# Attention with a pooled branch, then a two-layer network: early output by transposes into one bf16 bank, the band mask added in PSUM, a new set of planner costs

## The chip, the cores and the metric

The kernel runs on one core of one Trainium2 chip. Times are device microseconds of one execution; lower is better. Engines are called by their profile names: PE (TensorE matmul), PEld (its weight loads), DVE (VectorE), ACT (ScalarE), POOL (GpSimd), SP (SyncE, which issues DMAs).

## The reference

Eight batches of eight heads, 576 positions, 64 channels. Each head has a local attention (each position sees the positions less than 4 away) and an attention over q, k and v averaged in groups of four, whose output is repeated four times. The two are added, the heads joined, and a two-layer network follows on all 4608 tokens.

```python
q_d = q.reshape(B, H, Sd, 4, D).mean(axis=3)          # k_d, v_d alike; Sd = 144
out_up = np.repeat(sm_attn(q_d, k_d, v_d), 4, axis=2)
mask = np.abs(pos[:, None] - pos[None, :]) < 4
scores = np.where(mask, scale * q @ k.T, -1e9)
out_local = softmax(scores) @ v
x = (out_up + out_local).transpose(0, 2, 1, 3).reshape(4608, 512)
h = x @ w_in                                          # 512 -> 2048
out = (h - np.tanh(h)) @ w_out                        # 2048 -> 512
```

## The kernel before, in words

Work is split into 32 pairs of heads, p = 0 to 31, four to a batch (NP = 4), and nine dense blocks of 512 tokens.

For a pair, q and k are loaded in float32 (`qkn`), cast and reordered to bf16 (`qr`, lines 515 and 523), and transposed so that channels lie on partitions: for p < 12 on PE (line 547) with a copy to `qk` (551), from p = 12 on by a transposing DMA into `qT` and an ACT copy (534). Two additions, on DVE or POOL (564, 569), sum groups of four into `qkd`. Windows of v are cast to bf16 (`vw`, 451); v is pooled by a matmul with `pick` for p < 12 and by POOL (472, 476) from then on.

The scores stand in PSUM. The local ones are made in five tiles of 120 or 96 queries by 128 keys (584): four tiles in the first two-bank buffer, t1, by `s1`; the fifth, with the pooled scores (606), in a second one, t2, by `s2`. From p = 12 on `s1` and `s2` are one operation. ACT takes exponentials into `E` (622 for t1; 634 and 637 for t2). For p < 4 the mask enters as a bias that PE adds (589). For the other 28 pairs DVE multiplies the exponentials, in SBUF, by a mask of ones and zeros (626 and 641). PE then multiplies `E` by v with a column of ones (650, 657), which gives the outputs and their sums in a third two-bank buffer; DVE takes the reciprocal (670) and scales (672) into `ln`, seven blocks: five local, two pooled.

What follows is the output step. For p < 12 (below `X_DMA`), `back` brings the channels to partitions and joins the parts on PE: three matmuls with the constant `up` spread each pooled column over four (683, 685), and six with the identity add the local part (692), all in a float32 buffer of two banks; a copy on DVE or ACT (720, 721) writes `xT`. From p = 12 on a transposing DMA on SP writes `lT`, and the `join`, two additions on DVE or POOL (703, 709), writes `xT`.

A dense block is 16 steps of `mm1` (734: four matmuls of 512 columns, then tanh on ACT, 742, and a subtraction on DVE into `gT`, 745) and 16 quarter steps of `mm2` (760: four matmuls each, sixteen for 128 rows of the result; then an ACT copy into `y`, 771, and a DMA out, 774). Steps of one block's `mm2` alternate with the next block's `mm1`.

The order is written by a planner. Each operation has an engine, a cost in ns, the things it reads and writes, and a priority; some have a choice of engine. `order` runs a list schedule with these costs, with latencies `LAT` after which another engine sees a result, and with eight PSUM banks of which a kind of work may hold so many (`cap`: attention "b" 6, dense "d" 4). On each engine the operation with the least priority number among the ready ones goes first; dense matmuls have 5000, attention 10p, so attention goes ahead of dense work on PE. The instructions of each engine then stand in a fixed order and wait by semaphores. Planned times aren't used on the chip. `filler` puts idle matmuls (911) in planned gaps of the start phase.

The exponential and the mask that follows it are these lines:

```python
op("ACT", 960, lambda: A.activation(
    out=e1, in_=two(t1)[:, :, 0:480], func=AF.Exp, scale=SCALE), drain=[t1], ...)
if p >= NP:
    op("DVE", 950, lambda: V.tensor_tensor(
        out=e1, in0=e1, in1=mask[:, 0:480].unsqueeze(1).to_broadcast([128, 2, 480]),
        op=ALU.mult), reads=["mask"], writes=[("E", e, 0)], pri=pri)
```

Of the kernel before, what the change touches and what calls it, by code (L numbers as in the profile page):

```python
# [23 lines left out]
class Program:  # L24

    LAT = {"PE": 270, "ACT": 150, "DVE": 110, "POOL": 150, "SP": 50, "DMA": 2200}
    RING = 230

    def __init__(self):
        self.ops = []  # L30
        self.alternatives = {}
        self.slack = []
        self.soon = set()
        self.goal = set()
        self.ring = {}
        self.rings = {}
        self.touch = []
        self.use = []
        self.toks = []
        self.cap = {}  # L40
        self.last_write = {}
        self.readers = {}
# [66 lines left out]
    def order(self):  # L109
# [56 lines left out]
        for i in range(n):  # L166
            if left[i] == 0:
                make_ready(i)
        for step in range(n):
            best = None  # L170
            for eng, cand in ready.items():
                if not cand:
                    continue
                now = max(free.get(eng, 0.0), min(at[i] for i in cand))
                if eng == "PE":
# [8 lines left out]
                else:  # L184
                    pick = min((self.ops[i][4], i) for i in cand if at[i] <= now)[1]
# [12 lines left out]
            end = now + self.ops[i][1]  # L198
            want = [t for t in self.use[i] if t.first == i]
# [57 lines left out]
def kernel(  # L257
# [9 lines left out]
    nc = tc.nc  # L267
# [31 lines left out]
    mask = fixed("mask", [128, 576], BF16)  # L299
# [19 lines left out]
    up = lT[1].rearrange("p n c -> p (n c)")[:, 0:S]  # L319
    r = fixed("r", [128, 2, 7], FP32, 2)  # L320
    ln = fixed("ln", [128, 7, 128], BF16, 2)
# [31 lines left out]
    def c_up():  # L353

        GP.memset(up, 1.0)
        GP.affine_select(out=up, in_=up, compare_op=ALU.is_ge, fill=0.0,
                         base=0, pattern=[[1, S]], channel_multiplier=-4)
        GP.affine_select(out=up, in_=up, compare_op=ALU.is_ge, fill=0.0,
                         base=3, pattern=[[-1, S]], channel_multiplier=4)

# [8 lines left out]
    def c_mask():  # L369

        GP.memset(mask, 1.0)
        m4 = mask[:, 0:480].rearrange("p (t c) -> p t c", c=QW)
        for part, pat in ((m4, [[0, 4], [1, QW]]),
                          (mask[:, 480:576], [[1, 96]])):
            neg = [[-s, n] for s, n in pat]
            GP.affine_select(
                out=part, in_=part, compare_op=ALU.is_ge, fill=0.0,
                base=-1, pattern=neg, channel_multiplier=1)
            GP.affine_select(
                out=part, in_=part, compare_op=ALU.is_ge, fill=0.0,  # L380
                base=7, pattern=pat, channel_multiplier=-1)
        GP.affine_select(
            out=mask[:, 0:QW], in_=mask[:, 0:QW], compare_op=ALU.is_ge,
            fill=0.0, base=-4, pattern=[[0, QW]], channel_multiplier=1)
        GP.affine_select(
            out=mask[:, 480:576], in_=mask[:, 480:576], compare_op=ALU.is_ge,
            fill=0.0, base=99, pattern=[[0, 96]], channel_multiplier=-1)
# [80 lines left out]
    def pool_v4(p):  # L468
# [9 lines left out]
        op("POOL", 1150, a1, reads=[("v4", s)], writes=["v2"], pri=10 * p - 12)  # L478
        op("POOL", 750, a2, reads=["v2"], writes=[("vp", s)], pri=10 * p - 12)

    def pool_v(hb):
# [15 lines left out]
        op("ACT", 590, lambda: A.copy(  # L497
# [5 lines left out]
    def attention(p):  # L503
# [10 lines left out]
        if p >= NEARLY:  # L514
            op("POOL", 1300, lambda: GP.tensor_copy(  # L515
# [14 lines left out]
        if p >= T_DMA:  # L530
            P.dma("SP", 1740, lambda: nc.sync.dma_start_transpose(
                out=qT[s], in_=qr[s].rearrange("p a c -> p (a c)")), 1300, 72,
                  src=[("qr", s, 0), ("qr", s, 1)], dst=[("qT", s)], pri=-50, lead=500)
            op("ACT", 1250, lambda: A.copy(  # L534
# [3 lines left out]
        else:  # L538
            for a0, a1, tn, cn in ((0, 5, 290, 740), (5, 9, 230, 620)):
# [10 lines left out]
                def copy(fn, a0=a0, a1=a1, b16=b16):  # L550
# [5 lines left out]
                          ("DVE", cn, lambda copy=copy: copy(V.tensor_copy))][:1 + (p < NP)],  # L556
# [10 lines left out]
        def add2(eng):  # L567
            with nc.allow_low_precision("pooled q and k"):
                eng.tensor_tensor(out=qkd[s][:, 0:G],  # L569
                                  in0=half[:, :, 0, :],  # L570
                                  in1=half[:, :, 1, :], op=ALU.add)
        P.choice([(name, n1, lambda eng=eng: add1(eng)) for name, n1, _, eng in adders],
# [41 lines left out]
        if new:  # L614
            op("PE", 620, s12, slack=late, reads=qks + [("qkd", s)], fill=[t1, t2], pri=pri)
        else:
            op("PE", 420 * cold + 250 * (p < NP), s1, slack=late,
# [4 lines left out]
        op("ACT", 960, lambda: A.activation(  # L622
            out=e1, in_=two(t1)[:, :, 0:480], func=AF.Exp, scale=SCALE),
           drain=[t1], writes=[("E", e, 0)], pri=pri)
        if p >= NP:
            op("DVE", 950, lambda: V.tensor_tensor(  # L626
                out=e1, in0=e1,
                in1=mask[:, 0:480].unsqueeze(1).to_broadcast([128, 2, 480]),
                op=ALU.mult), reads=["mask"], writes=[("E", e, 0)], pri=pri)
        yield  # L630
        if not new:
            op("PE", 380 * cold + 100 * (p < NP), s2, slack=late, reads=qks + [("qkd", s)],
               fill=[t2], pri=pri)
        op("ACT", 310, lambda: A.activation(  # L634
            out=e2v, in_=two(t2)[:, :, 0:96], func=AF.Exp, scale=SCALE),
           drain=[t2], writes=[("E", e, 1)], pri=pri)
        op("ACT", 650, lambda: A.activation(  # L637
            out=e3, in_=two(t2)[:, :, 96:384], func=AF.Exp, scale=SCALE / 16.0),
           drain=[t2], writes=[("E", e, 2)], pri=pri)
        if p >= NP:  # L640
            op("DVE", 450, lambda: V.tensor_tensor(  # L641
                out=e2v, in0=e2v,
                in1=mask[:, 480:576].unsqueeze(1).to_broadcast([128, 2, 96]),
                op=ALU.mult), reads=["mask"], writes=[("E", e, 1)], pri=pri)
# [25 lines left out]
        op("DVE", 200, lambda: V.reciprocal(out=r[s], in_=blocks()[:, :, :, 64]),  # L670
           drain=[to], writes=[("r", s)], pri=pri)
        op("DVE", 1060, lambda: V.tensor_tensor(  # L672
# [6 lines left out]
        tb = P.psum(2, kind)  # L679

        def back():
            for half in range(2):
                T.matmul(two(tb)[:, half, 0:288], ln[s][:, 5, :], up[:, 288 * half:288 * half + 288],
                         start=True, stop=False)
            T.matmul(two(tb)[:, 1, 224:288], ln[s][0:16, 6, :], up[0:16, 0:64],
                     start=False, stop=False)
            for t in range(NT):
                q0, q1 = QW * t, QW * t + NQ[t]
                for half in range(2):
                    c0, c1 = max(q0, 288 * half), min(q1, 288 * half + 288)  # L690
                    if c0 < c1:
                        T.matmul(two(tb)[:, half, c0 - 288 * half:c1 - 288 * half],  # L692
                                 ln[s][0:NQ[t], t, :], ident[0:NQ[t], c0 - q0:c1 - q0],
                                 start=False, stop=(t == (2, NT - 1)[half]))
        if p >= X_DMA:
            P.dma("SP", 1350, lambda: nc.sync.dma_start_transpose(
# [4 lines left out]
            def join(eng):  # L701
# [12 lines left out]
            P.choice([("DVE", 1900, lambda: join(V)), ("POOL", 1400, lambda: join(GP))],  # L714
                     reads=[("lT", s)], writes=[("x", b, j)], pri=pri)
            return
        op("PE", 450 * cold, back, slack=late, reads=[("ln", s), ("lT", 1), "ident"],
           fill=[tb], pri=pri)
        xs = xT[j][:, b * S:(b + 1) * S].rearrange("p (n c) -> p n c", n=2)
        P.choice([("DVE", 720, lambda: V.tensor_copy(out=xs, in_=two(tb)[:, :, 0:288])),  # L720
                  ("ACT", 680, lambda: A.copy(out=xs, in_=two(tb)[:, :, 0:288]))],
                 drain=[tb], writes=[("x", b, j)], pri=pri)
# [4 lines left out]
    def mm1(kb, fc):  # L727
# [14 lines left out]
        op("ACT", 590, lambda: A.activation(  # L742
            out=u[us], in_=one(tok), func=AF.Tanh),
           drain=[tok], writes=[("u", us)], pri=DPRI)
        op("DVE", 670, lambda: V.tensor_tensor(  # L745
# [6 lines left out]
    def mm2(kb, i):  # L752
        ts, part, g = i // 4, i % 4, kb % 2
        if part == 0:
# [190 lines left out]
```

The softmax here doesn't subtract the row's maximum and nothing guards it: scores larger than these inputs give would overflow.

## Time and profile before

| | us |
|---|---|
| median of 6 runs | 334.29 (331.36 to 335.60) |
| the profiled execution | 334.08, span 332.0 |
| PE busy | 317.8 (96%) |
| DVE busy | 211.6 (64%) |
| ACT busy | 202.6 (61%) |
| POOL busy | 176.6 (53%) |

The span goes from the first to the last instruction of the profiled execution; about 2 us of its own time lie around it. Busy times are of that execution. A matmul's busy time includes its way through the array, and the next one starts before it has ended, so a busy PE isn't PE at its best; idle PE time is certain. Until about 25 us the first batch's attention runs alone; dense matmuls go from 25.4 to 327.7 us, attention beside them until 249 us.

### The profile page before, as it was taken

Reading aid. Unit: us, or ns where it says so; the run is one execution under the profiler, and the core shown is the slowest. Engines: PE = TensorE matmul, PEld = TensorE weight load, DVE = VectorE, ACT = ScalarE, POOL = GpSimd, SP = SyncE. Lnnn points to the kernel's source line nnn. Section 1 sums busy time; section 2 is a strip of 40 time slices with the busy share of each in tenths; the row PEclk is TensorE's granted clock in tenths of the full one; section 3 lists DMA queues with packets and bytes.
Section 4 is the critical chain, followed back from the end, with each engine's and each line's share of the span. In section 5 each row is a group of like instructions: output and inputs, shape, how many; then the busy total and the mean of one; then the engine's idle time right before and its main releaser. Section 6 shows DMA issues by size and latency. Waiting matters only on the chain.

```text
span 332.0 us, 6546 instructions
## 1 busy us (share of the span) xinstructions
PE 317.8 (96%) x2461; PEld 158.6 (48%) x2461; DVE 211.6 (64%) x330; ACT 202.6 (61%) x334; POOL 176.6 (53%) x211
## 2 busy tenths in 40 slices
PE   7989999999999999999796999999999999999994
PEld 2554555564444544444443445444444444444441
DVE  4766764579967969777979868778754334443300
ACT  4878864588777866687764476868534443344411
POOL 8564448859667698879788848887310000000000
PEclk9999999999999999999999999999999999999999
DMA  7999999999999989999999999982320001000121
GB/s 235 252 244 206 250 253 229 315 307 220 251 261 259 248 189 241 259 215 239 237 244 230 270 224 255 199 214 61 91 59 34 32 33 64 32 32 32 37 92 64
DMA packets 108862, 59.80 MB, mean 180 GB/s; under 512 B 86174, under 2 KB 96030, under 8 KB 108830
## 3 DMA queue, kind: packets, MB, share of 16 engines
q1 hardware_dynamic: 104318, 54.60, 70.0%
q0 software_dynamic: 4224, 4.19, 7.7%
q10 hardware_dynamic: 288, 0.59, 0.6%
q8 instruction: 19, 0.31, 0.4%
q14 instruction: 13, 0.11, 0.1%
HBM read 43.64 MB, written 9.44 MB: 160 GB/s over the span
## 4 chain that ended last, share of the span: by engine, by line
PE 70%; DVE 13%; DMA 8%; ACT 3%; POOL 3%; issue 1%; SPq 1%; POOLq 0%; ACTq 0%
PE bank L760 32%; PE bank L734 28%; DMA vst<-in_v_dram 5%; DMA lT<-ln 3%; DVE E L626 3%; DVE E L641 3%; DVE ln L672 3%; PE bank L650 2%; PE bank L584 2%; DVE gT L745 2%; PE bank L657 2%; DVE xT L703 1%; ACT E L622 1%; PE bank L692 1%; PE bank L547 1%
## 5 line engine op out<-in xcount | busy, mean ns | idle before, releaser
L734 PE MATMUL bank<-xT,w_in_sb 128*128 128x512 bf16 x576 | 146.0, 379 | 0.3 <-DVE gT L745 0.3
L760 PE MATMUL bank<-w_out_sb,gT 128*128 128x512 bf16 x576 | 145.2, 379 | 0.0
L745 DVE TENSOR_TENSOR gT<-bank,u 128x512 bf16<-128x512 f32 x144 | 97.4, 685 | 63.3 <-ACT u L742 62.7
L742 ACT ACTIVATE u<-bank 128x512 f32<-128x512 f32 x144 | 86.0, 598 | 77.9 <-PE bank L734 75.3
L760 PEld LDWEIGHTS <-gT 128*128 128x128 bf16 x576 | 53.9, 98 | 62.0
L734 PEld LDWEIGHTS <-w_in_sb 128*128 128x128 bf16 x576 | 53.8, 98 | 62.0 <-issue 0.5
L564 POOL TENSOR_TENSOR half<-qk 128x576 f32<-128x576 bf16 x28 | 32.1, 1146 | 19.5 <-ACT qk L551 10.1
L515 POOL CAST qr<-qkn 128x1152 bf16<-128x1152 f32 x28 | 32.3, 1152 | 11.6 <-DMA qT<-qr 5.7
L622 ACT ACTIVATE E<-bank 128x960 bf16<-128x960 f32 x32 | 31.1, 972 | 11.9 <-PE bank L584 11.8
L626 DVE TENSOR_TENSOR E<-E,mask 128x960 bf16<-128x960 bf16 x28 | 30.3, 1082 | 11.3 <-ACT E L622 11.2
L672 DVE TENSOR_TENSOR ln<-bank,r 128x896 bf16<-128x896 f32 x32 | 34.7, 1087 | 0.9
L771 ACT COPY y<-bank 128x512 f32<-128x512 f32 x36 | 21.1, 587 | 19.6 <-PE bank L760 18.2
L451 POOL CAST vw<-vst 128x640 bf16<-128x640 f32 x31 | 25.3, 821 | 6.6 <-DMA vst<-in_v_dram 6.6
L472 POOL TENSOR_TENSOR v<-v 72x512 f32<-72x512 f32 x20 | 25.5, 1273 | 2.6 <-DMA v<-in_v_dram 1.9
L534 ACT COPY qk<-qT 128x1152 bf16<-128x1152 bf16 x20 | 24.1, 1204 | 1.7 <-DMA qT<-qr 1.7
L650 PE MATMUL bank<-vw,E 128*128 128x65 bf16 x320 | 20.1, 194 | 4.0 <-DVE E L641 2.2
L569 POOL TENSOR_TENSOR qkd<-half 128x288 bf16<-128x288 f32 x29 | 21.3, 735 | 1.3 <-DVE r L670 0.4
L650 PEld LDWEIGHTS <-E 128*128 128x128 bf16 x320 | 16.5, 98 | 11.1 <-DVE E L641 2.9
L476 POOL TENSOR_TENSOR vp<-v 72x256 bf16<-72x256 f32 x20 | 14.6, 732 | 12.8 <-PE bank L657 12.6
L637 ACT ACTIVATE E<-bank 128x576 bf16<-128x576 f32 x32 | 21.1, 660 | 0.0
L703 POOL TENSOR_TENSOR xT<-lT 128x480 bf16<-128x480 bf16 x11 | 11.1, 1010 | 15.3 <-DMA lT<-ln 15.2
L641 DVE TENSOR_TENSOR E<-E,mask 128x192 bf16<-128x192 bf16 x28 | 17.3, 618 | 0.7 <-ACT E L634 0.7
(75 smaller groups left out, 223.5 us busy)
## 6 DMA issues: line engine op xcount, KB each, us to landing
vst<-in_v_dram SPq DMA_DIRECT2D x62, 160.0 KB, 5.2
qkn<-in_q_dram SPq DMA_DIRECT2D x32, 288.0 KB, 5.7
out_dram<-y SPq DMA_DIRECT2D x36, 256.0 KB, 4.7
qkn<-in_k_dram SPq DMA_DIRECT2D x30, 288.0 KB, 5.8
v<-in_v_dram SPq DMA_DIRECT2D x20, 288.0 KB
w_in_sb<-in_moe_w_in_dram POOLq DMA_DIRECT2D x4, 512.0 KB, 13.1
w_out_sb<-in_moe_w_out_dram POOLq DMA_DIRECT2D x4, 512.0 KB, 9.1
qkn<-in_k_dram ACTq DMA_DIRECT2D x2, 288.0 KB, 3.3
```

Source lines behind the costliest of these rows:

```text
L472: GP.tensor_tensor(out=v2, in0=v4[s][:, :, :, 0:128], in1=v4[s][:, :, :, 128:256], op=ALU.add)
L515: op("POOL", 1300, lambda: GP.tensor_copy(out=qr[s].rearrange("p a (h d) -> p h a d", h=2), in_=qkn[sn].rearrange("p h (a d) -> p h a d", ...
L564: eng.tensor_tensor(out=half, in0=four[:, :, 0:2, :], in1=four[:, :, 2:4, :], op=ALU.add)
L622: op("ACT", 960, lambda: A.activation(out=e1, in_=two(t1)[:, :, 0:480], func=AF.Exp, scale=SCALE), drain=[t1], writes=[("E", e, 0)], pri=pri)
L626: op("DVE", 950, lambda: V.tensor_tensor(out=e1, in0=e1, in1=mask[:, 0:480].unsqueeze(1).to_broadcast([128, 2, 480]), op=ALU.mult), reads= ...
L641: op("DVE", 450, lambda: V.tensor_tensor(out=e2v, in0=e2v, in1=mask[:, 480:576].unsqueeze(1).to_broadcast([128, 2, 96]), op=ALU.mult), rea ...
L650: T.matmul(two(to)[:, hh, 65 * t:65 * t + 65], E[e][:, c:c + 128], vw[w][:, 2 * jj + hh, t, :], start=True, stop=True)
L672: op("DVE", 1060, lambda: V.tensor_tensor(out=ln[s].rearrange("p n (h d) -> p h n d", d=D), in0=blocks()[:, :, :, 0:64], in1=r[s].unsqueez ...
L734: T.matmul(one(tok), w_in_sb[:, dc, fc * 128:(fc + 1) * 128], xT[dc][:, kb * 512:kb * 512 + 512], start=(dc == 0), stop=(dc == N_DC - 1))
L742: op("ACT", 590, lambda: A.activation(out=u[us], in_=one(tok), func=AF.Tanh), drain=[tok], writes=[("u", us)], pri=DPRI)
L745: op("DVE", 670, lambda: V.tensor_tensor(out=gT[g][:, fc, :], in0=one(tok), in1=u[us], op=ALU.subtract), drain=[tok], reads=[("u", us)], w ...
L760: T.matmul(one(tok), gT[g][:, fc, ts * 128:ts * 128 + 128], w_out_sb[:, fc, :], start=(fc == 0), stop=(fc == N_FF - 1))
```

## The change

Six things change.

- For the 28 pairs p >= 4 the band is no longer multiplied into `E`. `bias` (0 in the band, -32768 outside) is added by DVE to the scores in PSUM, in place, before the exponential: one addition of 2 x 480 on t1, one of 2 x 96 on t2. `mask` is gone; POOL makes `bias` itself (`c_bias`).
- For p < 12 `back` is seven transposes on PE into one bank, read as bf16: five local blocks (576 columns) and two pooled ones (144). The pooled columns are copied into a new tile `od` by DVE or ACT, and DVE adds them, each spread over four, to the local ones from PSUM into `xT`. The constant `up` and `c_up` (three POOL operations) are gone.
- From p = 12 on the join may run on POOL only. Casts of v for p >= 4 may also run on ACT.
- Costs and latencies of the planner are new, and it keeps POOL apart from the DVE operations named in `port` (the additions 564 and 569).
- `s1` and `s2` are one operation from p = 8 on (`MERGE`). Results of `mm2` have a PSUM kind of their own, "y", with up to 3 banks.
- The last 128 rows of the last block are made in two halves of 256 columns, each with its own copy and DMA.

```diff
-    LAT = {"PE": 270, "ACT": 150, "DVE": 110, "POOL": 150, "SP": 50, "DMA": 2200}
+    LAT = {"PE": 235, "ACT": 145, "DVE": 110, "POOL": 140, "SP": 50, "DMA": 2000}
...
+                if eng == "DVE":
+                    now = max(free.get(eng, 0.0), min(
+                        max(at[i], port) if i in self.port else at[i] for i in cand))
+                elif eng == "POOL":
+                    now = max(now, port)
...
+            if eng == "POOL" or eng == "DVE" and i in self.port:
+                port = end
...
-    def c_mask():
+    def c_bias():
 
-        GP.memset(mask, 1.0)
+        GP.memset(bias, 0.0)
...
-        if new:
-            op("PE", 620, s12, slack=late, reads=qks + [("qkd", s)], fill=[t1, t2], pri=pri)
+        if p >= MERGE:
+            op("PE", 590, s12, slack=late, reads=qks + [("qkd", s)], fill=[t1, t2], pri=pri)
...
-        op("ACT", 960, lambda: A.activation(
+        def band(tok, lo, hi):
+            part = two(tok)[:, :, 0:hi - lo]
+            V.tensor_tensor(out=part, in0=part, in1=bias[:, lo:hi].unsqueeze(1)
+                            .to_broadcast([128, 2, hi - lo]), op=ALU.add)
+        if p >= NP:
+            op("DVE", 1080, lambda: band(t1, 0, 480), reads=["bias"], fill=[t1], pri=pri)
+        op("ACT", 860, lambda: A.activation(
...
         if p >= NP:
-            op("DVE", 950, lambda: V.tensor_tensor(
-                out=e1, in0=e1,
-                in1=mask[:, 0:480].unsqueeze(1).to_broadcast([128, 2, 480]),
-                op=ALU.mult), reads=["mask"], writes=[("E", e, 0)], pri=pri)
...
+            op("DVE", 280, lambda: band(t2, 480, 576), reads=["bias"], fill=[t2], pri=pri)
...
-        tb = P.psum(2, kind)
+        tb = P.psum(1, kind)
...
         def back():
-            for half in range(2):
-                T.matmul(two(tb)[:, half, 0:288], ln[s][:, 5, :], up[:, 288 * half:288 * half + 288],
-                         start=True, stop=False)
-            T.matmul(two(tb)[:, 1, 224:288], ln[s][0:16, 6, :], up[0:16, 0:64],
-                     start=False, stop=False)
...
+            for t in range(7):
+                q0, n = (QW * t, NQ[t]) if t < NT else (S + 128 * (t - NT), (128, 16)[t - NT])
+                T.transpose(flat()[:, q0:q0 + n], ln[s][0:n, t, :], ident[0:n, 0:n])
...
-            P.choice([("DVE", 1900, lambda: join(V)), ("POOL", 1400, lambda: join(GP))],
+            P.choice([("POOL", 1310, lambda: join(GP))],
...
-        P.choice([("DVE", 720, lambda: V.tensor_copy(out=xs, in_=two(tb)[:, :, 0:288])),
-                  ("ACT", 680, lambda: A.copy(out=xs, in_=two(tb)[:, :, 0:288]))],
-                 drain=[tb], writes=[("x", b, j)], pri=pri)
+        P.choice([("DVE", 130, lambda: V.tensor_copy(out=od[s], in_=flat()[:, S:S + G])),
+                  ("ACT", 170, lambda: A.copy(out=od[s], in_=flat()[:, S:S + G]))],
+                 drain=[tb], writes=[("od", s)], pri=pri)
+        op("DVE", 610, lambda: V.tensor_tensor(
+            out=xT[j][:, b * S:(b + 1) * S].rearrange("p (g a) -> p g a", a=4),
+            in0=flat()[:, 0:S].rearrange("p (g a) -> p g a", a=4),
+            in1=od[s].unsqueeze(2).to_broadcast([128, G, 4]), op=ALU.add),
+           drain=[tb], reads=[("od", s)], writes=[("x", b, j)], pri=pri)
...
-        op("DVE", 670, lambda: V.tensor_tensor(
+        op("DVE", 610, lambda: V.tensor_tensor(
             out=gT[g][:, fc, :], in0=one(tok), in1=u[us], op=ALU.subtract),
...
-        if part == 0:
-            ycur[0] = P.psum(1, "d")
+        split = kb == NBLK - 1 and ts == 3
+        if split:
+            cols, first, fcs = 256 * (part // 2), part % 2 == 0, 8
+        else:
+            cols, first, fcs = 0, part == 0, 4
+        if first:
+            ycur[0] = P.psum(1, "y")
...
+    MERGE = 8
...
-    T_QK, T_V, T_W, W_PRI, NEARLY = 800, 1000, 2850, 32, NP
-    CAST_V = [[("POOL", 820, GP.tensor_copy), ("ACT", 640, A.copy)],
-              [("POOL", 820, GP.tensor_copy)]]
+    T_QK, T_V, T_W, W_PRI, NEARLY = 760, 850, 3000, 32, NP
+    CAST_V = [[("POOL", 770, GP.tensor_copy), ("ACT", 620, A.copy)],
+              [("POOL", 770, GP.tensor_copy), ("ACT", 620, A.copy)]]
...
-    P.cap = {"b": 6, "d": 4}
+    P.cap = {"b": 6, "d": 4, "y": 3}
```

## The prediction, made before the changed kernel was run

> **What bounds the kernel now.** I read the page first (busy shares), then the table of windows, then what TensorE (PE) waits for, then the rows and spreads of the operations that the diff touches, and last the timeline of the worst stall. In the table of windows the columns are the window, its length, then busy time (instructions) of each engine, the clock and the DMA share.
>
> ```profile
> PE 317.8 (96%) x2461; PEld 158.6 (48%) x2461; DVE 211.6 (64%) x330; ACT 202.6 (61%) x334; POOL 176.6 (53%) x211
> ```
>
> ```profile
> 100.00:150.00 50.00, 49.45 (x388) 24.14 (x387) 40.04 (x56) 36.24 (x58) 40.12 (x45) 1.00 1.08 235
> 150.00:200.00 50.00, 45.47 (x371) 22.48 (x370) 40.93 (x55) 32.09 (x51) 39.53 (x43) 1.00 1.14 241
> 200.00:328.00 128.00, 127.68 (x767) 59.93 (x763) 63.18 (x94) 62.96 (x106) 30.36 (x36) 1.00 0.32 82
> sum 303.00, PE 296.95 PEld 146.28 DVE 195.96 ACT 185.67 POOL 159.46; mean PE 74.24 PEld 36.57 DVE 48.99 ACT 46.42 POOL 39.87
> ```
>
> The sum takes in 25 to 100 us as well. From 25 us, when the dense layers start, to 328 us PE is busy for 296.95 of 303 us, so the time after 25 us is PE's work plus about 6 us of holes, 4.5 of them between 150 and 200 us. In the timeline dense matmuls start 0.216 us apart; 1152 of them are 249 us, which no part of this change shortens. What can move is PE's attention work, the holes, the 25 us before and the 4 us after. Attention is not the bound: it ends before 249 us, and 80 us of dense work stand behind it.
>
> Who makes the holes (waits of PE from 25 to 328 us: total us, times, longest):
>
> ```profile
> PE bank L650 <- DVE E L641: 2.2, 2, 1.5
> PE bank L650 <- DVE gT L745: 1.1, 1, 1.1
> PE bank L606 <- POOL qkd L569: 1.1, 1, 1.1
> PE bank L650 <- DVE E L626: 0.5, 1, 0.5
> PE bank L683 <- DVE ln L672: 0.3, 1, 0.3
> PE bank L734 <- DVE gT L745: 0.3, 1, 0.3
> ```
>
> Five of the six are waits for VectorE (DVE), which is only 64% busy. The spreads (min/median/max ns, first and last start) say why:
>
> ```profile
> L626 DVE TENSOR_TENSOR E<-E,mask x28: 642/672/3476, 26.4 to 239.5; 128x960 bf16<-128x960 bf16 x28
> L641 DVE TENSOR_TENSOR E<-E,mask x28: 241/248/3804, 27.7 to 241.2; 128x192 bf16<-128x192 bf16 x28
> ```
>
> ```profile
> L703 DVE TENSOR_TENSOR xT<-lT x9: 646/1026/2992, 107.1 to 236.1; 128x480 bf16<-128x480 bf16 x9
> ```
>
> ```profile
> L745 DVE TENSOR_TENSOR gT<-bank,u x144: 627/691/693, 27.1 to 313.7; 128x512 bf16<-128x512 f32 x144
> ```
>
> Operations with both inputs in SBUF (the mask products L626 and L641, the join L703) stretch up to fifteen times; those with one input in PSUM (L745; L672 by its spread too, 1027 to 1093) never do. In the timeline (start us, us, engine, idle before) the longest stretch lies exactly beside a row of GpSimd (POOL) work:
>
> ```profile
> 177.16 1.01 POOL L703 TENSOR_TENSOR xT<-lT 128x480 bf16<-128x480 bf16 x1
> 177.20 3.80 DVE L641 TENSOR_TENSOR E<-E,mask 128x192 bf16<-128x192 bf16 x1
> ...
> 181.06 0.20 PE L650 MATMUL bank<-vw,E 128*128 128x65 bf16 x1 [1.54 <-DVE E L641]
> ```
>
> A 0.25 us product, begun 0.04 us behind a join on POOL, ends at 181.0, when POOL's unbroken row ends (join, two casts of v, a cast of qr until 180.9); PE, in order, stands behind it.
>
> **What the Trainium skill says.** "SBUF — State Buffer", section Who interferes with whom: DVE and GpSimd share one pair of SBUF ports as an exclusive lock; a DVE instruction with two SBUF inputs contends with a GpSimd instruction that reads SBUF, one with at most one SBUF input doesn't. The rows above agree: 3804 ns against 248 for the first kind, 693 against 691 for the second. "VectorE: DVE Perf Modes", The perf-mode tier table: tensor_tensor runs at 2x for bf16 in SBUF and at 1x with a PSUM operand. Agreed: 672 ns for 960 elements in SBUF, 1091 for 896 from PSUM. "TensorE: Matmul & The Clock Gate", Part 4: PE-mode transpose: about 275 ns in a kernel for a transpose; here L547 shows 219 ns for one and 56 ns from start to start, so the trace's spacing is used.
>
> **The change part by part.** All against the profiled execution: 334.08 us, of which the span is 332.0. The median of the runs is 334.29, so the difference carries over as it stands.
>
> 1. *Band added in PSUM (p >= 4).* L626 and L641 go: 30.3 + 17.3 = 47.6 us of DVE for 28 pairs, of which only 28 x (0.672 + 0.248) = 25.8 is their own work; 21.8 us is being locked out. In their place come two adds in PSUM before the exponentials. No row has DVE writing PSUM; the nearest are L672 (896 elements, 1087 ns) and L745 (512, 685), 1.05 ns an element: 960 elements 1.15 us, 192 elements 0.35, 42 us in all. Below: 1.0 us if a PSUM target is quicker; above: 1.3 if it is slower. So DVE gains only some 5 us of busy time, but the new operations have one SBUF input and can't be locked out. The chain per pair is now scores, add, exp, where it was scores, exp, mask: 1.15 + 0.35 against 0.67 + 0.25, 0.6 us longer undisturbed. That is covered by dense matmuls placed between; without this cover it would be 28 x 0.6 = 17 us.
>
> 2. *Joins on POOL alone (p >= 12).* The nine on DVE (9 x (1415 + 705) = 19 us) leave; POOL gets 9 x (1.01 + 0.35) = 12 us, and may give v casts (0.73 us each) to ScalarE (ACT). DVE has then no operation with two SBUF inputs after the start phase. Holes that hang on it: 2.2 + 1.1 (gT queued behind the 2.99 us join at 156.7) + 0.5 + 0.3 (gT behind a 2.25 us L626 at 81.8) = 4.1. Of the 1.1 for qkd, 0.4 is the same lock from the other side: that L569 took 1.08 us where 0.67 is usual. Together 4.5 us go.
>
> 3. *Early output (p < 12).* The old form is nine matmuls:
>
> ```profile
> 44.15 0.41 PE L683 MATMUL bank<-lT,ln 128*128 128x288 bf16 x2
> 44.49 0.20 PE L685 MATMUL bank<-lT,ln 16*128 16x64 bf16 x1
> 44.62 0.43 PE L692 MATMUL bank<-ident,ln 120*128 120x120 bf16 x6
> 44.89 0.38 PE L760 MATMUL bank<-w_out_sb,gT 128*128 128x512 bf16 x1
> ```
>
> From 44.15 to the next dense matmul at 44.89 it takes 0.74 us of PE. The new seven transposes: four of 120 columns at 53 ns from start to start (as in L692), one of 96 at 45, one of 128 at 56, and the one of 16 rows. Around the old 16-row matmul some 0.1 us is lost on each side, since its weights aren't loaded ahead (0.13 from L685 to L692, where 64 columns need 0.03); the new one keeps that, so about 0.22 with its own columns. Sum 0.53; bounds 0.36 (nothing lost) to 0.74 (no gain). I take 0.21 us saved, 8 x 0.21 = 1.7 us beside dense work. Evacuation: one copy of 576 (DVE 758 ns, ACT 639, six each) becomes a copy of 144 (about 0.2 by L551's 491 ns for 640 and 414 for 512) and a DVE add of 576 (0.75 by L745's slope). DVE gets 12 x 0.75 + some 2 - 4.5 = 6 us, ACT loses up to 4. The x tile is ready some 0.1 us later than before; the next dense block has other work ahead of it, except at p < 4, where the start phase waits for it. It is about even there.
>
> 4. *Start.* c_up, three POOL operations from 5.0 to 7.1 us, is gone; a cast of qr on POOL waited for their end until 7.33 and PE waited for it. The bias comes from POOL without the DVE step (0.31), so is no later. With four early outputs 0.2 us shorter in PE, I count -0.2 net; bounds -1 to +1, as the order is new and loads are at the DMA limit (share above 1.1).
>
> 5. *The last stretch of rows split in halves.* PE's work is the same within 0.1 us. The last copy shrinks from 512 to 256 columns: 587 ns to about 0.39 (ACT takes 336 for 192), and the last transfer is half (SP issues 37 of them for 36). 0.3 us saved; bounds 0.2 to 1, as 3.4 us pass from its issue at 328.4 to the end.
>
> 6. *Order from new times, scores fused from p = 8, second cap for y banks.* Nothing is added to PE. The old costs were durations as the page has them; the new ones are nearer to spacings (exp 860 against starts 867 apart in the trace; L745 610 against 601), and latencies are shorter, so attention is placed in PE's queue with less room to spare. Something late then stands in PE's way. Loads are the likeliest, since a landing takes 5 to 6 us in the median. I charge 1.0 us of new holes; below 0, above 7.
>
> Sum: 334.1 - 4.5 - 1.7 - 0.2 - 0.3 + 1.0 = 328.4 us.
>
> **Rivals.**
>
> A. *The holes form again elsewhere.* The chain before the exponential is longer, the planner trusts its times more, and PE waits 4.5 us for other things (E, loads, qkd). For: half of the holes were one-off pile-ups, and a new order has new ones. Against: the lock was the only unpredictable cost on DVE, and the planner never knew of it. Only 3, 4 and 5 remain of the gain: 334.1 - 2.2 = 331.9.
>
> B. *A fuller gain.* With DVE predictable nearly all 6 us of holes go, the 16-row transpose costs nothing (0.38 saved, 3.0 in all), and the start gains 1: 334.1 - 6 - 3.0 - 1 - 0.5 = 323.6. Against: a new order without any hole is rare.
>
> C. *Slower: POOL's queue holds attention up.* POOL is at 40 of 50 us in both windows above, and it gets all joins, each of which stands in its queue until the transposed output lands:
>
> ```profile
> POOL xT L703 <- DMA lT<-ln: 15.2, 6, 7.0
> ```
>
> Six of eleven joins already held POOL for 15.2 us. Behind a waiting join are the next pair's qr, half, qkd and vp, and PE's scores wait for qkd. If each of the nine moved joins holds PE for its own 1.36 us, 12 us are lost against the forecast: 340.6. From 5.7 us of such waits on the kernel is slower than before, from 9 by over 1%. Against: PE waits for POOL after 25 us just once now, and casts can leave for ACT.
>
> D. *DVE's adds don't help*, because a PSUM target at 1.3 us and DVE at 80% between 100 and 200 make DVE late anyway: part of A by its time, 332.
>
> **How the numbers follow.** Forecast 0.50 (325.5 to 330.5), A with D 0.20, B 0.12, C 0.18. A 1% change, about what can be told from none here, is 3.3 us. Below 331.0 lie nearly all of the forecast, B and a small part of A: 0.63. Above 337.6 lies most of C: 0.15. Between is 0.22. The range drops the outer half of B and the outer part of C: 321.5 to 335.5.
>
> **What would show it.** Right: L626 and L641 replaced by DVE adds whose maximum stays within 0.1 us of their median; PE's holes between 150 and 200 us under 2 us; early outputs near 0.53 us from their first transpose to the next matmul; waits of PE for DVE near 1 us in total. Wrong: PE's busy time after the start shrinking by less than 1 us, waits of PE for POOL or for loads above 5 us, adds that reach 2 us, or a dense start later than 26.5 us.

## The result and the profile after

The changed kernel takes 337.31 us in the median (335.18 to 339.60), against 334.55 for the kernel before. The ratio is 1.0101, interval 1.0083 to 1.0119: slower by 1%, where 328.4 us was forecast. The profiled execution has a span of 337.9 us against 332.0. At 339.60 us it was the slowest of the 33, while the one before, at 334.08, lies near its median; so the 6 us between the two traces are more than the 2.8 between the medians.

The busy shares of the changed kernel, then its table of windows (columns as before the change):

```profile
PE 318.5 (94%) x2450; PEld 160.8 (48%) x2450; DVE 193.7 (57%) x320; ACT 204.0 (60%) x348; POOL 173.3 (51%) x216
```

```profile
25.00:100.00 75.00, 73.38 (x673) 39.51 (x672) 51.17 (x80) 53.43 (x100) 44.77 (x49) 1.00 1.15 248
100.00:150.00 50.00, 48.58 (x422) 24.70 (x419) 37.36 (x58) 38.00 (x62) 42.47 (x51) 1.00 1.13 245
150.00:200.00 50.00, 44.53 (x356) 21.65 (x355) 28.53 (x45) 31.90 (x53) 38.92 (x46) 1.00 1.12 251
200.00:240.00 40.00, 37.64 (x305) 18.50 (x304) 26.56 (x40) 28.37 (x48) 29.30 (x36) 1.00 0.70 145
240.00:334.00 94.00, 94.00 (x467) 44.33 (x466) 33.74 (x49) 37.07 (x63) 1.44 (x3) 1.00 0.12 45
sum 309.00, PE 298.12 PEld 148.69 DVE 177.36 ACT 188.76 POOL 156.90; mean PE 59.62 PEld 29.74 DVE 35.47 ACT 37.75 POOL 31.38
```

DVE lost 18 us of busy time, and PE has still not gained. Its holes after 25 us went from 6 us (303 - 296.95) to 10.9 (309 - 298.12), all before 240 us, while attention runs. The rest of the ledger is small: the first dense matmul starts at 26.1 us for 25.4, and from the last matmul's end to the end of the span it takes 3.4 us for 4.4. From the first dense matmul to the end of the last there are 308.3 us for 302.3: some 5 of these 6 us are holes, and the rest is busy time, which rose by 1.2 us after 25 us (298.12 for 296.95) where the forecast had it shrink. This rise probably belongs to the holes as well: a dense matmul is 379 ns long and the next one usually starts 216 ns after it, so in front of a hole some 0.16 us more shows as busy, and 17 holes over 0.25 us for 7 make an estimated 1.6 us.

What PE waits for, from 25 to 334 us (total us, times, longest):

```profile
PE bank L608 <- POOL qkd L570: 4.5, 4, 1.6
PE bank L657 <- ACT E L642: 1.4, 4, 0.3
PE bank L764 <- DMA w_out_sb<-in_moe_w_out_dram: 1.0, 1, 1.0
PE bank L731 <- DVE gT L742: 0.9, 3, 0.4
PE bank L650 <- ACT E L630: 0.5, 2, 0.4
```

The waits for the mask products are gone. In their place PE waits for POOL (pooled scores, 608, want `qkd`), for exponentials and for a load of weights. The operations that were to change did change as forecast; the band's adds (56, of two sizes) and the early output in the timeline:

```profile
L626 DVE TENSOR_TENSOR bank<-bank,bias x56: 353/750/1167, 26.7 to 237.6; 128x960 f32<-128x960 f32 x28, 128x192 f32<-128x192 f32 x28
```

```profile
70.94 0.60 PE L687 MATMUL bank<-ident,ln 120*128 120x120 bf16 x7
71.47 0.60 PE L764 MATMUL bank<-w_out_sb,gT 128*128 128x512 bf16 x2
```

No add exceeds 1167 ns (by form the means are 1157 and 356), and seven transposes take 0.53 us from the first to the next matmul (70.94 to 71.47). The eight early outputs beside dense work take 0.52 to 0.53 us each in this way, 4.2 in all, where the kernel before took 0.75 to 0.84 and 6.2.

How the longest wait for `qkd` comes about, in the timeline (start, length, engine; idle before in brackets):

```profile
216.48 1.01 POOL L696 TENSOR_TENSOR xT<-lT 128x480 bf16<-128x480 bf16 x1 [2.38 <-DMA lT<-ln]
217.45 0.35 POOL L702 TENSOR_TENSOR xT<-lT 128x96 bf16<-128x96 bf16 x1
217.75 0.73 POOL L477 TENSOR_TENSOR vp<-v 72x256 bf16<-72x256 f32 x1
218.56 1.26 POOL L473 TENSOR_TENSOR v<-v 72x512 f32<-72x512 f32 x1
219.78 1.15 POOL L565 TENSOR_TENSOR half<-qk 128x576 f32<-128x576 bf16 x1
221.01 0.67 POOL L570 TENSOR_TENSOR qkd<-half 128x288 bf16<-128x288 f32 x1
...
221.73 0.30 PE L608 MATMUL bank<-qkd 64*128 64x144 bf16 x4 [1.64 <-POOL qkd L570]
```

POOL stood 2.38 us before a join whose transposed output hadn't landed, then worked through its queue, and PE reached the scores 1.64 us before `qkd`. It looks like rival C. But the same row of waits has exponentials and a weight load in it, which no join explains. That left three theories.

### The profile page after: what moved, and what is told of

Its sections match the earlier page's. It is cut to its first block, busy times and chain, and to the rows that moved or that the text cites. A ratio compares the mean times of both kernels' runs of the same rounds, so it can differ in the third digit from the quotient of the medians.

```text
span 337.9 us, 6569 instructions
## 1 busy us (share of the span) xinstructions
PE 318.5 (94%) x2450; PEld 160.8 (48%) x2450; DVE 193.7 (57%) x320; ACT 204.0 (60%) x348; POOL 173.3 (51%) x216
## 4 chain that ended last, share of the span: by engine, by line
PE 35%; POOL 10%; DMA 7%; issue 4%; SPq 2%; ACT 2%; DVE 0%; POOLq 0%; ACTq 0%
PE bank L764 19%; PE bank L731 15%; DMA vst<-in_v_dram 4%; POOL half L565 2%; POOL xT L696 2%; DMA lT<-ln 2%; POOL v L473 2%; POOL qr L516 2%; DMA qT<-qr 1%; POOL qkd L570 1%; SPq L402 1%; POOL vp L477 1%; POOL xT L702 1%; PE bank L650 1%; PE bank L657 1%
## 5 line engine op out<-in xcount | busy, mean ns | idle before, releaser
L764 PE MATMUL bank<-w_out_sb,gT 128*128 128x512 bf16 (+1 forms) x592 | 144.9, 373 | 1.4 <-DMA w_out_sb<-in_moe_w_out_dram 1.0
L764 PEld LDWEIGHTS <-gT 128*128 128x128 bf16 x592 | 55.7, 98 | 62.9 <-issue 2.3
L626 DVE TENSOR_TENSOR bank<-bank,bias 128x960 f32<-128x960 f32 (+1 forms) x56 | 41.2, 757 | 10.4 <-PE bank L586 7.8
L565 POOL TENSOR_TENSOR half<-qk 128x576 f32<-128x576 bf16 x29 | 33.2, 1146 | 23.6 <-ACT qk L552 15.4
L696 POOL TENSOR_TENSOR xT<-lT 128x480 bf16<-128x480 bf16 x20 | 20.2, 1012 | 22.7 <-DMA lT<-ln 22.5
L776 ACT COPY y<-bank 128x512 f32<-128x512 f32 (+1 forms) x37 | 21.3, 575 | 15.6 <-PE bank L764 15.6
L473 POOL TENSOR_TENSOR v<-v 72x512 f32<-72x512 f32 x20 | 25.4, 1268 | 1.3 <-DMA v<-in_v_dram 0.2
L570 POOL TENSOR_TENSOR qkd<-half 128x288 bf16<-128x288 f32 x30 | 20.0, 667 | 3.0 <-DVE half L565 2.4
L642 ACT ACTIVATE E<-bank 128x576 bf16<-128x576 f32 x32 | 21.4, 668 | 0.2
L452 POOL CAST vw<-vst 128x640 bf16<-128x640 f32 x19 | 13.8, 724 | 6.8 <-DMA vst<-in_v_dram 6.8
L452 ACT CAST vw<-vst 128x640 bf16<-128x640 f32 x13 | 9.7, 743 | 11.6 <-DMA vst<-in_v_dram 11.6
L586 PE MATMUL bank<-qk 64*128 64x120 bf16 (+1 forms) x320 | 15.8, 216 | 0.9 <-ACT E L630 0.5
## 6 DMA issues: line engine op xcount, KB each, us to landing
w_in_sb<-in_moe_w_in_dram POOLq DMA_DIRECT2D x4, 512.0 KB, 11.1
```

The costliest lines, as they stand in the source:

```text
L473: GP.tensor_tensor(out=v2, in0=v4[s][:, :, :, 0:128], in1=v4[s][:, :, :, 128:256], op=ALU.add)
L565: eng.tensor_tensor(out=half, in0=four[:, :, 0:2, :], in1=four[:, :, 2:4, :], op=ALU.add)
L626: V.tensor_tensor(out=part, in0=part, in1=bias[:, lo:hi].unsqueeze(1) .to_broadcast([128, 2, hi - lo]), op=ALU.add)
L696: eng.tensor_tensor(out=x0.rearrange("p (t g a) -> p t g a", t=4, a=4), in0=lT[s][:, 0:4, 0:QW].rearrange("p t (g a) -> p t g a", a=4), in ...
L764: T.matmul(one(tok)[:, 0:n], gT[g][:, fc, ts * 128:ts * 128 + 128], w_out_sb[:, fc, cols:cols + n], start=(fc == 0), stop=(fc == N_FF - 1))
```

## The experiments

Theory 1: the new planner times are too short, so attention stands in PE's queue ahead of what it needs; 1a says it is the DMA times, 1b the compute costs. Theory 2: joins on POOL alone hold its queue up. Theory 3: every new order has its own pile-ups, and the numbers mean nothing. "a_" kernels are the changed one with an edit, "b_" kernels the one before with an edit. Each ratio is to runs of the kernel before made beside it. b_newcost, a_engold, a_latold, b_dmanew, a_loadold, a_dvejoin and b_band have four runs, the others 12 to 20.

**All costs, and room on PE.**

a_oldcost sets back all costs that both kernels have; b_newcost gives the new ones to the kernel before. Two lines of some 45 numbers:

```diff
-    LAT = {"PE": 235, "ACT": 145, "DVE": 110, "POOL": 140, "SP": 50, "DMA": 2000}
+    LAT = {"PE": 270, "ACT": 150, "DVE": 110, "POOL": 150, "SP": 50, "DMA": 2200}
...
-    T_QK, T_V, T_W, W_PRI, NEARLY = 760, 850, 3000, 32, NP
+    T_QK, T_V, T_W, W_PRI, NEARLY = 800, 1000, 2850, 32, NP
```

> The changed kernel, with every planner cost and latency that both kernels have set back to the value of before (LAT, engine costs, load and transpose costs); band, transposes, join on POOL, fused scores and the y cap stay. Theory 1 (new costs leave attention too little room in PE's queue): waits of PE for POOL and ACT after 25 us fall from 6.9 to under 3.5 us, time near 332 to 334. Theory 2 (joins on POOL alone hold qkd up behind late transposes): waits for qkd stay at 3 to 5 us, time 336 to 338. Theory 3 (each new order has its own pile-ups): time anywhere from 331 to 339, with waits at other places.

> The kernel before with the new planner costs and latencies for all operations it has, nothing else changed. Theory 1: the same loss without the rest of the change, 3 to 6 us over before (337 to 340), with new waits of PE for POOL, ACT or loads. Theory 2: within 1 us of before. Theory 3: 331 to 339.

The other two change one constant, which adds to the planner's time of readiness of PE's attention operations:

```diff
-    M2_FIRST, T_DMA, X_DMA, NEW, LATE = 16, 12, 12, 12, 0
+    M2_FIRST, T_DMA, X_DMA, NEW, LATE = 16, 12, 12, 12, 1000
```

> The changed kernel with LATE = 1000: the planner counts 1 us more before any attention operation of p >= 8 on PE, so it stands later among the dense matmuls; nothing else is changed. Theory 1: waits of PE after 25 us fall from 10.5 us to under 4 and the time from 337.3 to about 330. Theory 2: POOL's lateness against plan is 1 to 2 us, so it falls by half, to 333. Theory 3: about 331, and other kernels with such room gain the same.

> The kernel before with LATE = 1000 alone. Theory 1: the old costs had this room already for what can be planned, and the port lock (up to 3.8 us) is longer than 1 us, so it gains 1 to 2 us, 332 to 333. Theory 2: the same. Theory 3: 331 to 332, as much as the changed kernel gains.

Measured: a_oldcost 331.56 us, 0.9937 (0.9912 to 0.9961); b_newcost 342.52, 1.0255 (1.018 to 1.033); a_late1000 336.45, 1.0061 (1.0034 to 1.0089); b_late1000 334.43, 1.0002 (0.9966 to 1.0037). The costs alone slow the old kernel by 2.5%, more than the 337 to 340 us of theory 1 and outside the 331 to 339 of theory 3; without them the changed kernel is 0.6% faster than before. Theory 1 has both signs right, and theory 2 isn't needed. A microsecond of room isn't enough: it gave 0.9 us where 7 were expected, and nothing in the kernel before, where 1 to 2 were.

**Which costs.**

a_dmaold sets the DMA times back, a_engold the compute costs, a_latold the three compute latencies. The DMA times are of three sorts: `T_QK`, `T_V` and `T_W` are what the plan counts for the transfer of a load, 1740, 1350 and 530 what it counts on SP for issuing a transpose or an output, and 2200 the latency of a landing:

```diff
-    LAT = {"PE": 235, "ACT": 145, "DVE": 110, "POOL": 140, "SP": 50, "DMA": 2000}
+    LAT = {"PE": 235, "ACT": 145, "DVE": 110, "POOL": 140, "SP": 50, "DMA": 2200}
-            P.dma("SP", 1340, lambda: nc.sync.dma_start_transpose(
+            P.dma("SP", 1740, lambda: nc.sync.dma_start_transpose(
-            P.dma("SP", 1260, lambda: nc.sync.dma_start_transpose(
+            P.dma("SP", 1350, lambda: nc.sync.dma_start_transpose(
-            P.dma("SP", 440, lambda: nc.sync.dma_start(
+            P.dma("SP", 530, lambda: nc.sync.dma_start(
-    T_QK, T_V, T_W, W_PRI, NEARLY = 760, 850, 3000, 32, NP
+    T_QK, T_V, T_W, W_PRI, NEARLY = 800, 1000, 2850, 32, NP
```

> The changed kernel with only the planner's DMA times set back: loads 800, 1000 and 2850, the two transposes 1740 and 1350, the output 530, landing latency 2200. Theory 1a (loads and transposes are planned too early, POOL stands in line for them): the waits of PE for POOL's qkd (4.5 us) and for E go, time 332 to 334. Theory 1b (the compute costs are the ones that are too small): 336 to 338, qkd waits stay. Theory 3 (each new order has its own pile-ups): 331 to 339.

The other two, a_engold by two of its lines:

```diff
-        op("ACT", 860, lambda: A.activation(
+        op("ACT", 960, lambda: A.activation(
-        op("ACT", 490, lambda: A.activation(
+        op("ACT", 590, lambda: A.activation(
```

```diff
-    LAT = {"PE": 235, "ACT": 145, "DVE": 110, "POOL": 140, "SP": 50, "DMA": 2000}
+    LAT = {"PE": 270, "ACT": 150, "DVE": 110, "POOL": 150, "SP": 50, "DMA": 2000}
```

> The changed kernel with only the planner's costs of operations on ACT, DVE, POOL and PE set back (exp 960, 310, 650; scale 1060; tanh 590; subtraction 670; casts, pooling and join on POOL by some 50 to 140 more); latencies and DMA times stay new. Theory 1a: 336 to 338. Theory 1b: 332 to 334. Theory 3: 331 to 339.

> The changed kernel with only the planner's latencies of PE, ACT and POOL set back (270, 150, 150). They differ by 35, 5 and 10 ns, so by theories 1a and 1b the time stays within 1% of the changed kernel, 335 to 339; by theory 3 even so small a difference gives another order and a time anywhere from 331 to 339.

Measured: a_dmaold 332.66, 0.9951 (0.9919 to 0.9983); a_engold 342.29, 1.0241 (1.0188 to 1.0295); a_latold 341.54, 1.0236 (1.017 to 1.0302). This points to the DMA times (1a). Setting the compute costs back made it worse by over 1%, and so did a change of latencies by 5 to 35 ns, which 1a had put within 1%; both lie outside the range of theory 3 too. Theory 3 is right in that one order differs from another, by 4 to 5 us here, as much as the DMA times gave; so more orders are needed, and follow below.

The waits of PE in a_dmaold, the first lines:

```profile
PE bank L764 <- DVE ln L672: 1.0, 1, 1.0
PE bank L657 <- ACT E L642: 0.8, 1, 0.8
PE bank L586 <- ACT y L776: 0.6, 1, 0.6
```

The 4.5 us for `qkd` are gone, though all joins still run on POOL. What POOL itself waits for the transposed outputs fell too; first a_dmaold, then the changed kernel (their traces are of a run 1.4 us below the median and of one 2.3 above):

```profile
POOL xT L696 <- DMA lT<-ln: 11.2, 4, 6.7
```

```profile
POOL xT L696 <- DMA lT<-ln: 22.5, 12, 6.0
```

**The DMA times alone, and further back.**

b_dmanew is the kernel before with the DMA times of the changed one (the diff above, reversed). a_slowdma goes on from a_dmaold:

```diff
-    T_QK, T_V, T_W, W_PRI, NEARLY = 800, 1000, 2850, 32, NP
+    T_QK, T_V, T_W, W_PRI, NEARLY = 880, 1100, 2850, 32, NP
```

> The kernel before with only the planner's DMA times of the changed kernel (loads 760, 850, 3000; transposes 1340 and 1260; output 440; landing latency 2000), everything else as before. Theory 1a (loads and transposes planned too early): 339 to 343, as with all new costs. Theory 3 (each new order has its own pile-ups): 331 to 339.

> The changed kernel with the DMA times of before, and the loads a tenth slower still in the plan (880 for q and k, 1100 for a window of v). Theory 1a: attention is planned later again, the last waits for E and ln from 150 us on go, 329 to 332. Theory 3: 330 to 338.

b_dmanew takes 346.76, 1.0328 (1.0266 to 1.0389), above the 339 to 343 expected: these numbers alone are enough for a loss, and for more than that of the whole change. In its trace PE waits for `qkd` again, with joins still free to run on DVE:

```profile
PE bank L606 <- POOL qkd L569: 4.5, 8, 1.3
PE bank L650 <- DVE E L641: 3.4, 5, 1.1
```

a_slowdma takes 334.40, 0.9989 (0.9960 to 1.0017), a miss: its dense start moved from 26.2 us in a_dmaold to 28.6, and PE is busy for 69.7 of the 75 us from 25 to 100 where a_dmaold has 73.4, though after 100 us it has fewer holes (2.4 us for 5.1 up to 240). Its trace is of its fastest run, 331.82. In this order, planning attention later cost at the start what it gained behind.

Why too early costs can be read from the planner's own start times, which the program computes while it is built, against the trace. How late the 31st of the 32 big exponentials starts on the chip:

| kernel | us late | median, us |
|---|---|---|
| a_slowdma | 1.7 | 334.40 |
| a_dmaold | 4.1 | 332.66 |
| a_oldcost | 4.8 | 331.56 |
| before | 5.6 | 334.55 |
| a_late1000 | 11.1 | 336.45 |
| b_dmanew | 15.6 | 346.76 |
| changed kernel | 15.7 | 337.31 |

Over all twenty kernels it is 11.1 to 21.4 us late wherever DMA times are new, wholly or in part, and 1.7 to 7.5 elsewhere. Lateness alone doesn't give the time: b_dmanew and the changed kernel are equally late and 9.5 us apart.

From the 13th to the last of these exponentials the plan counts 6.66 us a pair in the changed kernel and 7.07 in a_dmaold; on the chip both took 7.35. So the shorter times made the plan faster and not the work. Between 100 and 200 us the DMA share is 1.08 to 1.14 in the kernels before and after, which suggests that loads and transposes set this pace; no run isolates it. One of the times could have been read in the trace before, as SP's issue of the transpose of q and k (min/median/max ns), planned at 1740 and then at 1340:

```profile
L531 SPq DMA_TRANSPOSE qT<-qr x20: 1312/2177/4182, 73.2 to 216.7; - x20
```

A plan that believes in faster transfers places attention earlier in PE's queue; the data comes when it comes, and PE, which takes its instructions in order, stands.

**Loads or transposes.** The diff of a_dmaold in two parts: its line of `T_QK, T_V, T_W` alone, and all but that line.

> The changed kernel with only the three load times set back (800, 1000, 2850); transposes, output and landing latency stay new. If the loads are the DMA times that matter: 331 to 334. If the transposes and the latency are: 336 to 342.

> The changed kernel with the two transposes (1740, 1350), the output (530) and the landing latency (2200) set back, the loads' times new. If the loads are what matters: 336 to 342. If the transposes and the latency are: 331 to 334.

a_loadold 338.95, 1.0144 (1.0086 to 1.0201); a_trold 336.40, 1.0058 (1.003 to 1.0087). Neither part alone does it, against both expectations; only both together gave 332.7. The same exponential is 12.7 and 13.7 us late in them. Waits for `qkd` are down to 0.2 and 0.7 us there, so these waits were one form of the loss and not its cause.

**The join.**

```diff
-            P.choice([("POOL", 1310, lambda: join(GP))],
+            P.choice([("DVE", 1900, lambda: join(V)), ("POOL", 1310, lambda: join(GP))],
```

> The changed kernel with the DMA times of before and the join free to run on DVE as well. Theory 2 (joins on POOL alone cost time): faster than with POOL alone, 330 to 331.5. The prediction's view (a join on DVE can be locked out by POOL, and DVE's queue behind it): 333 to 336, with waits of PE for gT or ln behind joins of 2 to 3 us.

> The changed kernel with the join free to run on DVE again, DMA times new. If joins on POOL alone are a cause of their own: 333 to 335, with the waits for qkd gone. If the early plan of the loads is the cause: 336 to 343, the waits only moving to DVE's queue.

> The changed kernel with all planner costs and latencies of before and the join free to run on DVE: the two settings that gained, together. If they add up: 329 to 331. If the join's gain was chance of the order: 331 to 334.

a_dvejoin 339.07, 1.0154 (1.0088 to 1.0221): with the new DMA times, joins on DVE don't help, and the waits move to DVE's queue, as theory 1 had it (PE waits 7.1 us for `gT`). So theory 2 falls as the cause. With the old times, a_dmaold_dvejoin takes 330.68, 0.9876 (0.985 to 0.9902), the fastest of all: theory 2's 330 to 331.5 came true, and the prediction's view, 333 to 336, did not, although 13 joins ran on DVE and the longest was stretched to 3.76 us. But a_oldcost_dvejoin takes 332.17, 0.9944 (0.9916 to 0.9971), no better than a_oldcost. That joins gain on DVE is therefore not settled; a_dmaold_dvejoin as it stands beats both kernels, the one before by 1.2% and, by way of it, the changed one by about 2.2% (0.9876 / 1.0101).

**By chance.**

```diff
-    LAT = {"PE": 235, "ACT": 145, "DVE": 110, "POOL": 140, "SP": 50, "DMA": 2200}
+    LAT = {"PE": 240, "ACT": 145, "DVE": 110, "POOL": 140, "SP": 50, "DMA": 2200}
```

> The changed kernel with the DMA times of before and the latency of PE 240 for 235 in the plan, a change without meaning that gives another order. It measures what an order is worth by chance: theory 1a expects 330 to 335, near the 332.7 without it; theory 3 anything up to 339.

332.94, 0.9936 (0.9905 to 0.9967), beside 0.9951 without it. With the DMA times of before, the five orders of the changed kernel a_oldcost, a_dmaold, a_dmaold_n and the two with joins on DVE lie within 2.3 us (330.7 to 332.9); a_slowdma, with slower loads still, takes 334.4. With the new ones, the partial sets counted, the spread over seven orders is larger (336.4 to 342.3), and all of it is above. So chance of the order is not enough to explain the difference.

**The parts of the structure alone, in the kernel before.**

b_trans is the early output by transposes (the pooled columns are copied into free columns of `lT`). b_band is the add in PSUM with the mask products gone. b_band_n is b_band with PE's latency at 275. The edits of b_trans are the lines of the change at `tb`, `back`, `od` and `c_up`; those of b_band:

```diff
+        if p >= NP:
+            op("DVE", 1080, lambda: band(t1, 0, 480), reads=["bias"], fill=[t1], pri=pri)
         op("ACT", 960, lambda: A.activation(
             out=e1, in_=two(t1)[:, :, 0:480], func=AF.Exp, scale=SCALE),
...
-        if p >= NP:
-            op("DVE", 950, lambda: V.tensor_tensor(
-                out=e1, in0=e1,
...
+        if p >= NP:
+            op("DVE", 280, lambda: band(t2, 480, 576), reads=["bias"], fill=[t2], pri=pri)
```

> The kernel before with the early output by seven transposes, one bank, the small copy and the DVE add, and nothing else changed (the copied pooled columns use free columns of lT). By the prediction: 1.7 to 2 us less of PE, 332 to 333. By theory 3 the new order covers this up: 331 to 338.

> The kernel before, with the band added in PSUM and the mask products gone, and nothing else changed; the joins on DVE stay. By the reasoning of the prediction: the waits of PE for the mask products (2.7 us) go, the adds show 1157 and 356 ns, holes of 1 to 2 us behind joins on DVE stay, 331.5 to 333. If the longer chain before the exponential counts: no gain, 334 to 336, with waits of PE for ACT's E.

> The kernel before with the band added in PSUM, as in b_band, and PE's latency 275 for 270 in the plan: another order by a change without meaning. If the 4 to 5 us that b_band lost belong to the band itself: 336 to 340, with waits of PE for gT again. If they belong to that one order (gT queued on DVE behind two joins that wait for a transpose): 331 to 335.

b_trans 332.85, 0.9923 (0.9896 to 0.9949): 1.7 to 2 us expected, 2.1 measured by the medians and 2.6 by the ratio; `c_up` is gone in it too. b_band 338.51, 1.0137 (1.009 to 1.0185), and b_band_n 337.55, 1.0088 (1.0062 to 1.0114): the band alone costs 1.4% and 0.9%, in two orders, where a gain was expected. Each trace shows a place. DVE's timeline in b_band_n:

```profile
140.41 3.83 DVE L701 TENSOR_TENSOR xT<-lT 128x480 bf16<-128x480 bf16 x1 [1.75 <-DMA lT<-ln]
144.16 1.70 DVE L707 TENSOR_TENSOR xT<-lT 128x96 bf16<-128x96 bf16 x1
145.79 2.47 DVE L743 TENSOR_TENSOR gT<-bank,u 128x512 bf16<-128x512 f32 x4
```

and PE's wait:

```profile
PE bank L732 <- DVE gT L743: 5.9, 3, 5.2
```

The join on DVE, two inputs in SBUF, waits for its transpose, is stretched to 3.83 and 1.70 us (0.65 and 0.25 undisturbed), and four `gT` stand behind it, without which PE can't go on. In b_band it is another thing: no join takes more than 1.32 us, but joins on DVE wait 19.0 us for transposes (3.4 in the kernel before), and PE waits 6.2 us for `gT`. Why the band costs time here stays open: a_oldcost_dvejoin has the band in PSUM, joins on DVE that wait 13.7 us for transposes and the old costs, and takes 332.17. It also has the transposes, the scores fused from p = 8, the cap "y" and the planner's `port`, and no run separates these.

## Why the prediction was wrong

The forecast was 328.4 us, the time 337.3. Two terms make up most of these 9 us: step 2 booked 4.5 us, of which nothing measurable came, and step 6 charged 1.0 us for what cost 4.7.

- *What bounds it* was right: after 25 us the time is PE's work plus holes, and attention has slack behind it. The loss is in the holes.
- *Step 1, the band*: its sizes were right (1157 and 356 ns against 1.15 and 0.35 us; never stretched). The cover for the longer chain was too light a claim: PE waits for `E` (operations at 650 and 657) about 2.6 us in the changed kernel, where the mask chain had 2.7. About half of it goes with the DMA times: in a_dmaold it is 1.2 us.
- *Step 2, 4.5 us from the lock*, is a term that failed. The waits named did go. But this counted holes as if the order stayed: each removed wait was booked as a gain, although the change writes a new order. In the orders with the old DMA times and joins on POOL alone the whole structure gave 1.6 to 2.2 us (0.9951, 0.9936 and 0.9937 of 334.5), about what steps 3 to 5 give by their measured sizes (2.0 less 0.7, and 0.9). The one order that gave more, a_dmaold_dvejoin with 4.1 us, still has the lock on its joins.
- *Step 3* was right: 0.53 us each, 1.7 us forecast; the eight early outputs beside dense work went from 6.2 to 4.2 us of PE.
- *Step 4* was off by 1 us and within its bounds: dense start at 26.1 us for 25.4. The first loads are issued in the same order, but the second pair's q is there only at 8.1 us (6.9 before); PE waits 1.76 us for its cast, and from 8.9 to 12.0 us the granted clock is 0.50 (1.00 before), with nine transposes at 1.12 us for 0.68. That alone doesn't explain the start: in a_dmaold the cast begins at 6.6 us, the clock is 1.00, and the dense start is 26.2 too. The cause stays open.
- *Step 5*: 0.9 us gained for 0.3.
- *Step 6* is the other term that failed, by its size. I charged 1.0 us for the new times, and gave 7 as the bound above. They cost 4.7 us in the changed kernel (337.3 to 332.7 with the DMA times set back), 12 in the kernel before. I had compared the compute costs with spacings, found them nearer to the trace, and let that stand for all the numbers. The DMA times went down as well (all but that of the weights), and no line of the trace was read for these: the DMA share was above 1.1, a landing took 5 to 6 us, and the issue of a transpose 2.18 us in the median, where the plan went from 1.74 to 1.34. Times that are too short err all to one side; jitter, which I priced, does not.
- *Rival C* had the place right (POOL's queue, joins, `qkd`) and named the wrong cause: with the old DMA times the same joins on POOL let PE wait for `qkd` no more. Rival A's result, holes that form again elsewhere, is what happened, with more than it allowed.
- *Its own signs*: PE's busy time after the start didn't shrink, and waits for POOL and for loads came to 5.5 us (4.5 and 1.0), both signs of being wrong. The adds and the dense start stayed within theirs.

Open: why loads alone or transposes alone, set back, recover nearly nothing; why the band alone costs time in the kernel before; and whether the join gains on DVE.

## What to carry to other kernels

Where a written order feeds in-order queues, hold the planner's times for a busy resource against what the trace shows of it. Shorter ones didn't speed it up here (7.35 us a pair with both sets); they put waiting work in front of work that could run. Before booking a removed wait as a gain, ask whether the order stays the same; if not, two or three orders that differ by a constant without meaning tell what an order is worth by itself: here 0.3 us with the old DMA times (a_dmaold_n), 4.2 with the new ones (a_latold). And a lock that shows in the trace need not be worth its waits: the fastest kernel here still has it.

## What the runs showed of the hardware

- The Trainium skill's rule on shared ports ("SBUF — State Buffer", Who interferes with whom) held here: adds with one input in PSUM and one in SBUF kept within 1167 ns in 28 pairs, while joins with two SBUF inputs on DVE went from 0.65 to 3.83 us (b_band_n), the length of several POOL operations on end.
- DVE's adds that write PSUM in place cost here what it costs to write SBUF: 1157 ns for 960 elements and 356 for 192, where the line through 685 ns for 512 and 1087 for 896 elements into SBUF gives 1154 and 350.
- A transpose of 16 rows behind one of 128 starts 0.15 us after it, and the next matmul 0.11 us after that, where its 16 columns explain almost nothing; four of 120 take 0.05 each. The loads of the weights of these two matmuls start only 5 ns before them, those of the others some 50 ns (71.2 to 71.5 us in the changed kernel).
